# Who turns q and k, how fast the weights are rounded, and the order of the last outputs: seven edits to an attention and Fourier-mixing kernel

## The chip, the cores and the metric

The kernel runs on one core of one Trainium2 chip. The metric is the device time of one execution in microseconds (us). A core has five engines that run side by side [...]: TensorE (PE in the profile) multiplies matrices, VectorE (DVE), ScalarE (ACT) and GpSimd (POOL) do elementwise work, and SyncE (SP) issues the DMA transfers. Each engine takes its instructions in program order, so one that waits holds up everything queued behind it on the same engine.

## The reference, cut to what matters

Two stages follow each other. The first is block-sparse attention over 4 batches of 8 heads, 768 positions and 64 features per head; the mask lets a query block of 32 positions see its neighbours, the first and last block, and three random blocks.

```python
scores = scale * np.matmul(q, k.transpose(0, 1, 3, 2))
scores = np.where(mask, scores, -1000000000.0)
attn = np.exp(scores - np.max(scores, axis=-1, keepdims=True))
attn = attn / (np.sum(attn, axis=-1, keepdims=True) + 1e-09)
attn_out = np.matmul(attn, v)
x = attn_out.transpose(0, 2, 1, 3).reshape(B, S, H * D)      # 4 x 768 x 512
u = x + np.real(np.fft.fft(np.fft.fft(x, axis=1), axis=2))
un = (u - mean(u)) / np.sqrt(var(u) + 1e-06)                 # over the 512 columns
out = u + np.maximum(un @ w_ch1, 0.0) @ w_ch2                # 512 -> 2048 -> 512
```

The two weight matrices arrive as 64-bit floats.

## The kernel before, in words

**Attention.** The heads are taken two at a time: `pairs` is 4 batches of 4 pairs, 16 in all. A pair has 12 units (two halves of the queries, six chunks of 128 keys). `slot(sl)` is the loop body and takes two units, so a pair takes six slots, a batch (a *phase*) 24, and the attention 96. In a slot, `scores` makes S = K Q^T for its two units on TensorE (line 570), `weigh` makes the exponentials on ScalarE (line 590), and `values` multiplies the exponentials of the slot before with v (line 633). Exponentials live in four buffers (`ep`), so one must be used up before the exponential four units later can be written.

**The mask** comes in two ways. Early units are in `by_pe`: two more small bf16 products per unit, of `factors["at"]`, add a large negative number to the scores (line 580). Later units multiply the exponentials by a stored mask on VectorE (line 595). The switch is made by `go()` in `begin`, when the Fourier mixing of batch 0 is under way.

**The sums of the softmax** are made by TensorE in phase 0 (`add_up`, line 701). From phase 1 on `gather` adds up exponentials, either in one VectorE instruction (line 614) or in two GpSimd instructions (line 619). The two buffers it adds into are the ones that hold the two factors of the mask in phase 0; that is why `keep_factors`, in slot 19 (`sl == SB - 5`), first copies the factors into another buffer, room 2 of six (`room(i, ...)`). Before, two DMA transfers do this (line 479). Every later use of the factors reads the copy.

**Turning q and k.** The scores need q and k with the features on the partitions. Pairs up to number 4 are turned on TensorE (`turn`, line 503) and copied out of PSUM by ScalarE (lines 506, 512). Pairs from `BY_VECTOR` on (5 before) are loaded in blocks of 32 (`load_blocks`), turned by VectorE in one instruction each (`flip_blocks`, line 537) and, for q, put into order by six ScalarE copies (`in_order`, line 545). These steps stand at the end of the slot's work.

**The weights** come in 32 chunks of 128 x 512 64-bit words. A chunk is loaded into one of the six rooms (`w_load`, line 441) and rounded by two ScalarE instructions (lines 450, 453) and five VectorE instructions (lines 454, 456, 459, 461, 462). `w_steps` rounds chunks until `W_PACE * sl` are done, 1.42 a slot before, so that the last is done in slot 23; rooms 0 and 1 are wanted for the mixing afterwards.

**Mixing and channels.** `mixer` and `fourier` make the second stage of a batch while the next batch's attention runs. The steps stand in a queue, `apart`, and the large products in another, `late`. A small model of the engines' clocks (`when`, `busy`) decides at every `gap` how many of these steps are put between the attention's instructions. In `apart` are the division by the sums (line 743), the folding of x (lines 766 to 794, on VectorE), the products with the cosine and sine tables (lines 814 to 871), and the transposes back (`un_flip`, line 958). A step names the PSUM banks that it needs: `m` has two, `t` one; a capital `M` means both of `m`. The last batch makes its outputs in `outputs` (seven products a tile, line 1152) and stores them with `store` (line 1100).

The lines that carry the prediction:

```python
    BY_VECTOR = NP + 1                       # NP = 4
    W_PACE = 1.42
    ROOMS = 6
    def w_load(i):
        t = room(i % ROOMS, [P, 3 * WN], "wraw", U32)
    def w_steps(sl):
        while state["w"] < min(len(wchunks), W_PACE * sl):
            w_round(state["w"])
```

Of the kernel before, what the change touches and what calls it, by code (L numbers as in the profile page):

```python
# [102 lines left out]
def kernel(  # L103
# [14 lines left out]
    nc = tc.nc  # L118
# [91 lines left out]

    BY_VECTOR = NP + 1

    def load_blocks(n, a, tile):

# [219 lines left out]
    def room(i, shape, name, dtype=FP32):  # L436
        return big.tile(shape, dtype, tag=f"big{i}", name=name)

    def w_load(i):
        t = room(i % ROOMS, [P, 3 * WN], "wraw", U32)  # L440
        nc.sync.dma_start(out=t[:, 0:2 * WN].bitcast(I32), in_=wchunks[i][0])
        wraw[i] = t

# [25 lines left out]

    by_pe = set()
    factors = {"at": (of_k, off_q)}

    def keep_factors():

        kept = room(2, [P, 2, S], "factors", BF16)
        for a, t in enumerate(factors["at"]):
            nc.sync.dma_start(out=kept[:, a, :], in_=t)
# [104 lines left out]
    def weigh(u, s):  # L584
        n, w = divmod(u, UP)
        half, c = divmod(w, C)
        e = ep.tile([P, 2, HS], FP32, tag="e", name="e")
        e_of[u] = e
        if u in by_pe:
            nc.scalar.activation(out=e, in_=s[:, :, 0:HS], func=ACT.Exp, scale=scale)  # L590
            e_at[u] = busy("ACT", 0.8, max(s_at[u], e_free.pop(u - 2 * SLOT, 0.0))) + HOP
        else:
            nc.scalar.activation(out=s[:, :, 0:HS], in_=s[:, :, 0:HS], func=ACT.Exp, scale=scale)  # L593
            m = mask[:, c, half * HS:(half + 1) * HS].rearrange("p (o s) -> p o s", o=1)
            nc.vector.tensor_tensor(out=e, in0=s[:, :, 0:HS], in1=m.broadcast_to([P, 2, HS]),  # L595
                                    op=ALU.mult)
            e_at[u] = busy("DVE", 0.97, busy("ACT", 0.8, s_at[u]) + HOP) + HOP
            if n >= NP:
                gather(u)

    def gather(u):

# [20 lines left out]
    def values(u):  # L623
        n, w = divmod(u, UP)
        half, c = divmod(w, C)
        e = e_of[u]
        busy("PE", 0.75, e_at[u])
        vt = v_of[n]
        if c == 0:
            o_of[n, half] = ps_o.tile([P, HS], FP32, tag="o", name="o")  # L630
        o = o_of[n, half]
        for i in range(2):
            nc.tensor.matmul(o[D * i:D * i + D, :], vt[:, i, c, :], e[:, i, :],  # L633
                             start=(c == 0), stop=(c == C - 1))
        if u in by_pe and n >= NP:
            gather(u)
        if c == C - 1:
            if half == 1:
                v_of.pop(n)
            oT = sum_p.tile([P, HS], FP32, tag="oT", name="oT")  # L640
            if in_blocks(n):
                nc.vector.transpose(out=oT, in_=o_of.pop((n, half)))
                oT_at[n, half] = busy("DVE", 0.5, when["PE"] + HOP) + HOP
            else:
                nc.scalar.copy(out=oT, in_=o_of.pop((n, half)))
                oT_at[n, half] = busy("ACT", 0.5, when["PE"] + HOP) + HOP
            o_of[n, half] = oT
# [107 lines left out]
    def fourier(b, xA, xB, uns):  # L755
# [45 lines left out]
        def along(g):  # L801

            sa, sd, e1 = st["f"]
            if g == 0:
                st["zc"] = zc_p.tile([P, 2, KS], FP32, tag="zc", name="zc")
            ps = ps_m.tile([P, 512], FP32, tag="m", name="zp")
            odd = S // 4

            def cosine(ps, rows, cols):
                mm = nc.tensor.matmul
                for t in (0, 2):
                    mm(ps[rows, 0:KS], sa[:, t, cols], cs_sb[:, t, :], start=(t == 0), stop=False)  # L814
                mm(ps[rows, 0:odd], e1[:, cols], cs_sb[:, 1, 0:odd], start=False, stop=False)
                mm(ps[rows, odd:KS], sa[:, 1, cols], cs_sb[:, 1, odd:KS], start=False, stop=True)

            def keep_cosine(dst, ps):
                nc.scalar.copy(out=dst, in_=ps[:, 0:KS])

                nc.scalar.copy(out=_grid(dst, P + 1, 2, 63, 63, 1),
                               in_=_grid(ps, P, 2, 65, 63, 1))
                nc.scalar.copy(out=_run(dst, P, 2, P - 1), in_=_run(ps, P + 64, 2, -1))

            if g < 2:
                cosine(ps, slice(0, P), parts[g])
# [94 lines left out]
        def d(us, fn, *args):  # L921
# [7 lines left out]
        first += [("M" if g == 2 else "m", lambda g=g: along(g), 2.1, (1.0 if g < 2 else 0.5), 0.0)  # L929
                  for g in range(4)]  # L930
        pq = [("m", lambda m=m: across(m), 2.6 if m == 1 else 1.6, 0.7, 0.95) for m in range(T)]
        ar = [[d(1.4 if m == 1 and half == 1 else 1.0, arrive, half, m) for m in range(T)]
# [11 lines left out]
    def mixer(b, xA, xB):  # L944
# [6 lines left out]
        def un_flip(half, m):  # L951
            if half not in unT:
                unT[half] = tr_p.tile([P, ND, T * P], FP32, tag="tr", name="unT")
            un = uns.pop((half, m))
            tag, pool = (("t", ps_t), ("m", ps_m))[half]
            tp = pool.tile([P, ND, P], FP32, tag=tag, name="utp")
            for d in range(ND):
                nc.tensor.transpose(tp[:, d, :], un[:, d * P:(d + 1) * P], ident)  # L958
# [135 lines left out]
            if r == NF // 4 - 1:  # L1094
                store(half, m)

        def store(half, m):
            x = (xA, xB)[half]
            for p0, cnt, rows in _rows(out[b], T * half + m):
                nc.sync.dma_start(out=rows, in_=x[p0:p0 + cnt, m, :])  # L1100
            if m == T - 1:
                finished.add((b, half))

# [34 lines left out]
        def outputs(r, m, after):  # L1138
# [55 lines left out]
            ahead(4)  # L1194

        fl = [[("tm"[h], lambda h=h, m=m: un_flip(h, m), 0.6, 0.55, 0.0) for m in range(T)]
              for h in range(2)]

        before = first + [pq[0], ar[0][0], ar[1][0], sp[0][0],
# [44 lines left out]
    def do_apart():  # L1244
# [5 lines left out]
            return  # L1250
        done = state["ready"]
        if kind != "-":
            at = bank(kind.lower())
            done = busy("PE", pe, done) + HOP
        fn()
        if act:
# [7 lines left out]
    def gap(rest=0.0, ahead=None, kinds="tm"):  # L1264
# [4 lines left out]
        while apart:  # L1269
# [7 lines left out]
                if max(when["DVE"], state["ready"]) + dve > when["PE"] + rest + ahead:  # L1277
                    break
            elif kind != "-":
                bank_at = (max if kind == "M" else min)(free[kind.lower()])  # L1280
                if kind.lower() in used or max(state["ready"], bank_at) > when["PE"] + 0.1:
                    break
                used += kind.lower()
            do_apart()
        for item in list(short):
            kind, ready, fn = item
# [36 lines left out]
        return True  # L1323

    def w_loads():
        while state["got"] < min(len(wchunks), state["w"] + ROOMS):
            w_load(state["got"])
            state["got"] += 1

# [5 lines left out]
    def slot(sl):  # L1335
# [101 lines left out]
        while short and (not more or soon) and (  # L1437
# [159 lines left out]
```

## Time and profile before

| | |
|---|---|
| time, median of 3 | 1080.54 us (1080.32 to 1081.24) |
| span of the profiled execution | 1079.5 us |
| TensorE busy | 1042.1 us, 97% |
| VectorE busy | 661.5 us, 61% |
| ScalarE busy | 376.4 us, 35% |
| GpSimd busy | 227.4 us, 21% |
| mean granted TensorE clock | 0.991 |
| DMA, mean | 44 GB/s, but 177 to 239 GB/s in the first four fortieths |

The profile's page gives busy times, a strip of 40 slices and the costliest groups. A busy TensorE is an upper bound, since matmuls overlap and their ends are modelled. A share over the whole span hides that the stages differ: VectorE is 61% busy over all, but 95% in the first 100 us, in which the weights are rounded. The page's list of waits names, for each engine, which line of which engine ended its idle time.

### The profile page before, as it was taken

To read this page: it belongs to the slowest core of one execution; us is meant where nothing else is said; L and a number is where in the kernel's file an instruction comes from. 1 tells how busy PE (TensorE), PEld (TensorE's weight loads), DVE (VectorE), ACT (ScalarE), POOL (GpSimd) and SP (SyncE) were. 2 spreads that over 40 slices of the span, in tenths; PEclk is the share of its full clock that TensorE was granted. 3 is DMA by queue.
4 is the path that set the end of the run, shared out by engine and by line. 5 is a ranking of instruction groups with operands and counts; after the bars stand their busy time and mean duration, and the time that the engine had idled before them with its cause. 6 is when DMAs were issued, how large, how long until landed. Compare 5 with 4: busy or idle time off the path is not lost.

```text
span 1079.5 us, 12378 instructions
## 1 busy us (share of the span) xinstructions
PE 1042.1 (97%) x4378; PEld 537.1 (50%) x4378; DVE 661.5 (61%) x1226; ACT 376.4 (35%) x742; POOL 227.4 (21%) x256
## 2 busy tenths in 40 slices
PE   8999789999999999999999999999999999999996
PEld 4433234444455545444444555444444555568575
DVE  5899494777763634764568446665557255675663
ACT  5998555564311202443451302343320212210210
POOL 1000062323600001265454000354630001000000
PEclk9999899999999999999999999999999999999998
DMA  7757222221000001222211000212000001000001
GB/s 224 220 177 239 69 45 44 45 45 30 15 0 1 1 0 30 59 39 42 52 29 31 1 0 18 64 29 39 14 9 7 0 1 30 29 1 1 1 19 43
DMA packets 120769, 47.04 MB, mean 44 GB/s; under 512 B 108142, under 2 KB 113532, under 8 KB 120700
## 3 DMA queue, kind: packets, MB, share of 16 engines
q1 hardware_dynamic: 118812, 45.38, 17.1%
q10 hardware_dynamic: 1856, 0.79, 0.3%
q8 instruction: 36, 0.59, 0.2%
q14 instruction: 33, 0.27, 0.1%
q0 software_dynamic: 32, 0.01, 0.0%
HBM read 37.11 MB, written 6.29 MB: 40 GB/s over the span
## 4 chain that ended last, share of the span: by engine, by line
PE 90%; DVE 6%; issue 2%; ACT 1%; DMA 0%; POOL 0%; SPq 0%; ACTq 0%; POOLq 0%; DVEq 0%
PE y L1089 23%; PE z L1033 15%; PE s L570 12%; PE o L633 11%; PE yp L1033 8%; PE yy L1152 6%; PE xp L1033 4%; PE zp L843 2%; PE sp L701 1%; PE s L580 1%; PE zp L814 1%; PE tp L503 1%; PE utp L958 1%; PE sp L715 1%; PE xt L657 1%
## 5 line engine op out<-in xcount | busy, mean ns | idle before, releaser
L619 POOL TENSOR_TENSOR acc<-acc,e 128x384 f32<-128x384 f32 x154 | 156.8, 1055 | 212.2 <-ACT e L590 137.6
L570 PE MATMUL s<-qT,kT 64*128 64x384 f32 x768 | 154.3, 517 | 7.7 <-DVE kT L537 4.5
L633 PE MATMUL o<-e,vr 128*64 128x384 f32 x768 | 142.8, 500 | 0.0
L1092 DVE TENSOR_TENSOR x<-y,x 128x512 f32<-128x512 f32 x72 | 49.7, 690 | 133.1 <-PE y L1089 133.0
L1089 PE MATMUL y<-w_sb,hA 128*128 128x512 f32 x288 | 129.3, 596 | 1.7 <-ACT zs L845 1.7
L1089 PE MATMUL y<-w_sb,hB 128*128 128x512 f32 x288 | 128.5, 596 | 1.0 <-DVE x L1092 1.0
L595 DVE TENSOR_TENSOR e<-s,mask 128x768 f32<-128x768 f32 x98 | 89.0, 950 | 54.2 <-ACT s L593 48.5
L570 PEld LDWEIGHTS s<-qT,kT 64*128 64x128 f32 x768 | 64.6, 187 | 82.8 <-issue 26.1
L593 ACT ACTIVATE s<-s 128x768 f32<-128x768 f32 x98 | 74.3, 791 | 84.2 <-PE s L570 83.9
L1033 PE MATMUL z<-unT,t 128*128 128x384 f32 x256 | 93.2, 487 | 0.3 <-DVE hA L1038 0.3
L1089 PEld LDWEIGHTS y<-w_sb,hB 128*128 128x128 f32 x288 | 53.4, 190 | 67.7 <-issue 65.3
L590 ACT ACTIVATE e<-s 128x768 f32<-128x768 f32 x94 | 71.2, 812 | 42.6 <-PE s L580 38.6
L1089 PEld LDWEIGHTS y<-w_sb,hA 128*128 128x128 f32 x288 | 53.0, 190 | 65.5 <-issue 58.8
L906 POOL TENSOR_SCALAR st<-st 128x1 f32<-128x1 f32 x24 | 8.3, 348 | 358.8 <-DVE st L905 358.8
L633 PEld LDWEIGHTS o<-e,vr 128*64 128x64 f32 x768 | 48.3, 137 | 71.0 <-issue 67.6
L1038 DVE TENSOR_TENSOR hA<-z,hA 128x384 f32<-128x384 f32 x64 | 35.7, 557 | 77.8 <-PE z L1033 77.8
L1042 ACT ACTIVATE hA<-hA 128x384 f32<-128x384 f32 x64 | 33.4, 523 | 120.4 <-DVE hA L1038 120.3
L619 POOL TENSOR_TENSOR acc<-e 128x384 f32<-128x384 f32 x40 | 42.9, 1094 | 111.9 <-PE sp L715 85.7
L1033 PEld LDWEIGHTS z<-unT,t 128*128 128x128 f32 x256 | 48.5, 190 | 34.7 <-DVE hA L1038 1.3
L1042 ACT ACTIVATE hB<-hB 128x384 f32<-128x384 f32 x64 | 33.5, 523 | 85.9 <-DVE hB L1038 85.9
L1053 ACT COPY hA<-xp 128x384 f32<-128x384 f32 x32 | 15.3, 479 | 113.0 <-PE xp L1033 113.0
L1033 PE MATMUL xp<-unT,w_sb 128*128 128x384 f32 x128 | 47.6, 494 | 2.6 <-DVE x L1092 2.6
(204 smaller groups left out, 1430.8 us busy)
## 6 DMA issues: line engine op xcount, KB each, us to landing
wraw<-in_moe_w_ch_dram SPq DMA_DIRECT2D x32, 512.0 KB
vr<-in_v_dram SPq DMA_DIRECT2D x30, 192.0 KB
qb<-in_q_dram SPq DMA_DIRECT2D x44, 96.0 KB
kb<-in_k_dram SPq DMA_DIRECT2D x44, 96.0 KB
x<-oT SPq DMA_DIRECT2D x192, 12.0 KB
out_dram<-x SPq DMA_DIRECT2D x16, 128.0 KB
out_dram<-x SPq DMA_DIRECT2D x8, 256.0 KB
qr<-in_q_dram SPq DMA_DIRECT2D x24, 64.0 KB
```

Source lines behind the costliest of these rows:

```text
L570: nc.tensor.matmul(s[:, i, 0:HS], kT[rows, c * P:(c + 1) * P], qT[rows, queries], start=True, stop=u not in by_pe)
L590: nc.scalar.activation(out=e, in_=s[:, :, 0:HS], func=ACT.Exp, scale=scale)
L593: nc.scalar.activation(out=s[:, :, 0:HS], in_=s[:, :, 0:HS], func=ACT.Exp, scale=scale)
L595: nc.vector.tensor_tensor(out=e, in0=s[:, :, 0:HS], in1=m.broadcast_to([P, 2, HS]), op=ALU.mult)
L619: nc.gpsimd.tensor_add(out=acc[:, i, :], in0=start[:, i, :], in1=e[:, i, :])
L633: nc.tensor.matmul(o[D * i:D * i + D, :], vt[:, i, c, :], e[:, i, :], start=(c == 0), stop=(c == C - 1))
L1033: nc.tensor.matmul(to, a[:, k, :], c[:, k, :], start=(k == 0), stop=(k == ND // 2 - 1))
L1038: tt(out=to, in0=ps, in1=a, op=ALU.add)
L1042: nc.scalar.activation(out=h, in_=h, func=ACT.Relu)
L1089: nc.tensor.matmul(y, hs[0, half][:, l, m * P:(m + 1) * P], w2_sb[:, 4 * r + l, :], start=(l == 0), stop=(l == 3))
L1092: nc.vector.tensor_tensor(out=x[:, m, :], in0=y, in1=x[:, m, :], op=ALU.add)
L1152: nc.tensor.matmul(ps, a[:, k, :], c[k // 2][:, k % 2, :] if isinstance(c, list) else c[:, k, :], start=(k == 0), stop=(k == 3))
```

## The change

Seven edits are made together.

1. The two factors of the mask are copied by GpSimd instead of by DMA.
2. VectorE turns q and k from pair 2 on instead of from pair 5 on.
3. The steps of such a turn are issued right after the slot's exponentials, ahead of the mixing's steps, instead of at the end of the slot.
4. The weights are rounded at 1.1 chunks a slot. The rounding then lasts beyond the slot in which rooms 0 to 2 are needed for other things, so the last six chunks use rooms 3, 4 and 5 alone.
5. Units whose mask comes from TensorE are gathered in the order of the units across the switch.
6. Two steps of the mixing take bank `t` instead of a second bank `m`: the `side` product, and the last transposes of the second half.
7. In `outputs` the product with `o_s[m, 4]` goes ahead of the one with `a22`, and the last tile's second half is stored in two pieces of columns.

```diff
-    BY_VECTOR = NP + 1
+    BY_VECTOR = 2
...
+    w_rooms = [i % ROOMS for i in range(26)] + [3, 4, 5, 3, 4, 5]
+    def w_free(i):
+        return all(w_rooms[k] != w_rooms[i] for k in range(state["w"], i))
     def w_load(i):
-        t = room(i % ROOMS, [P, 3 * WN], "wraw", U32)
+        t = room(w_rooms[i], [P, 3 * WN], "wraw", U32)
...
         for a, t in enumerate(factors["at"]):
-            nc.sync.dma_start(out=kept[:, a, :], in_=t)
+            nc.gpsimd.tensor_copy(out=kept[:, a, :], in_=t)
...
+            if n >= NP:
+                to_gather.append(u)
...
+            gather_to(u)
...
-        if u in by_pe and n >= NP:
-            gather(u)
+        gather_to(u)
...
-                side = ps_m.tile([P, 512], FP32, tag="m", name="side")
-                at = bank("m")
+                side, at = ps_t.tile([P, 512], FP32, tag="t", name="side"), bank("t")
...
-            tag, pool = (("t", ps_t), ("m", ps_m))[half]
+            tag, pool = (("t", ps_t), ("m", ps_m))[half == 1 and m != 1]
...
+            ends = r == 1 and after is None
+            if ends:
+                store(1, m, slice(DH, DM))
             ahead(2)
-            plus(b0, product(ps_s, "s", a22, rights[4]))
-            if r == 1:
-                store(1, m)
-            ahead(3)
             p3 = product(ps_m, "m", o_s[m, 4], block(r, 1, 1))
             plus(a1, p3)
             if r == 1:
                 store(0, m)
+            ahead(3)
             ahead(4)
+            plus(b0, product(ps_s, "s", a22, rights[4]))
+            if r == 1:
+                store(1, m, slice(0, DH if ends else DM))
...
-    W_PACE = 1.42
+    W_PACE = 1.1
...
         for u, ps in got:
             weigh(u, ps)
+        if BY_VECTOR <= n + 1 < len(pairs):
+            for at, fn, args in ((0, squares, (n + 1, 0)), (1, flip_blocks, (n + 1, 0)),
+                                 (2, in_order, (n + 1,)), (4, flip_blocks, (n + 1, 1)),
+                                 (5, squares, (n + 1, 1))):
+                if s == at:
+                    fn(*args)
...
-        if BY_VECTOR <= n + 1 < len(pairs):
-            for at, fn, args in ((0, squares, (n + 1, 0)), (1, flip_blocks, (n + 1, 0)),
-                                 (2, in_order, (n + 1,)), (4, flip_blocks, (n + 1, 1)),
-                                 (5, squares, (n + 1, 1))):
-                if s == at:
-                    fn(*args)
         w_loads()
         w_steps(sl)
```

More of the change, by code (lines that the diff above doesn't have):

```diff
@@ L463, in w_round @@
         busy("DVE", 3.0, busy("ACT", 1.2))
-    by_pe = set()
+    by_pe, to_gather = set(), deque()
     factors = {"at": (of_k, off_q)}
@@ L597, in weigh, with gather_to @@
             e_at[u] = busy("DVE", 0.97, busy("ACT", 0.8, s_at[u]) + HOP) + HOP
+            gather_to(u)
             if n >= NP:
                 gather(u)
+    def gather_to(u):
+        while to_gather and to_gather[0] <= u:
+            gather(to_gather.popleft())
     def gather(u):
@@ L928, in fourier @@
                  d(1.0, fold_1, 1), d(1.2, fold_2, 0), d(0.6, fold_2, 2), d(1.3, fold_2, 1)]
-        first += [("M" if g == 2 else "m", lambda g=g: along(g), 2.1, (1.0 if g < 2 else 0.5), 0.0)
+        first += [("mt" if g == 2 else "m", lambda g=g: along(g), 2.1, (1.0 if g < 2 else 0.5), 0.0)
                   for g in range(4)]
@@ L1095, in channels, with store @@
                 store(half, m)
-        def store(half, m):
+        def store(half, m, cols=slice(0, DM)):
             x = (xA, xB)[half]
-            for p0, cnt, rows in _rows(out[b], T * half + m):
-                nc.sync.dma_start(out=rows, in_=x[p0:p0 + cnt, m, :])
+            for p0, cnt, rows in _rows(out[b][:, cols], T * half + m):
+                nc.sync.dma_start(out=rows, in_=x[p0:p0 + cnt, m, cols])
             if m == T - 1:
@@ L1193, in outputs @@
                 store(0, m)
+            ahead(3)
             ahead(4)
-        fl = [[("tm"[h], lambda h=h, m=m: un_flip(h, m), 0.6, 0.55, 0.0) for m in range(T)]
+            plus(b0, product(ps_s, "s", a22, rights[4]))
+            if r == 1:
+                store(1, m, slice(0, DH if ends else DM))
+        fl = [[("tm"[h == 1 and m != 1], lambda h=h, m=m: un_flip(h, m), 0.6, 0.55, 0.0)
+               for m in range(T)]
               for h in range(2)]
@@ L1252, in do_apart @@
         if kind != "-":
-            at = bank(kind.lower())
+            at = bank(kind[0])
             done = busy("PE", pe, done) + HOP
@@ L1279, in gap @@
             elif kind != "-":
-                bank_at = (max if kind == "M" else min)(free[kind.lower()])
-                if kind.lower() in used or max(state["ready"], bank_at) > when["PE"] + 0.1:
+                bank_at = max(min(free[k]) for k in kind)
+                if (any(k in used for k in kind) or
+                        max(state["ready"], bank_at) > when["PE"] + 0.1):
                     break
-                used += kind.lower()
+                used += kind
             do_apart()
@@ L1325, in w_loads @@
     def w_loads():
-        while state["got"] < min(len(wchunks), state["w"] + ROOMS):
+        while state["got"] < len(wchunks) and w_free(state["got"]):
             w_load(state["got"])
```

## The prediction

> **What bounds the kernel now.** I read the page first: TensorE is busy 97% of the span, so time can only come from TensorE work removed or TensorE idle time removed.
>
> ```profile
> PE 1042.1 (97%) x4378; PEld 537.1 (50%) x4378; DVE 661.5 (61%) x1226; ACT 376.4 (35%) x742; POOL 227.4 (21%) x256
> PE   8999789999999999999999999999999999999996
> PEclk9999899999999999999999999999999999999998
> ```
>
> The strip shows idle time at the start (slice 1), in slices 5 and 6, and at the very end. TensorE's list of waits names the middle ones:
>
> ```profile
> PE s L580 <- DMA factors<-at_q: 9.2, 1, 9.2
> PE s L570 <- DVE kT L537: 4.5, 1, 4.5
> PE xp L1033 <- DVE x L1092: 2.6, 3, 1.8
> ```
>
> The first is the copy of the factors by DMA, the second a turned k that VectorE delivers late. After 165 us all waits together are under 9 us. The table of windows shows how the early stage is limited:
>
> ```profile
> 80.00:100.00 20.00, 19.61 (x137) 7.83 (x137) 19.02 (x48) 17.29 (x37) 0.00 (x0) 1.00 0.73 227
> 100.00:120.00 20.00, 10.84 (x63) 3.82 (x61) 10.41 (x23) 7.29 (x17) 0.00 (x0) 0.77 0.54 169
> 140.00:160.00 20.00, 17.82 (x109) 7.49 (x107) 17.66 (x26) 11.36 (x21) 15.38 (x12) 1.00 0.19 42
> ```
>
> (Columns: stretch, length, busy us of PE, PEld, DVE, ACT, POOL, then clock, DMA share, GB/s.) In phase 0 TensorE, VectorE and ScalarE are all 86 to 98% busy; at 140 us GpSimd joins and ScalarE relaxes. TensorE's timeline gives the two stalls:
>
> ```profile
> 37.10 1.56 PE L570 MATMUL s<-qT,kT 64*128 64x384 f32 x8
> ...
> 104.92 1.56 PE L570 MATMUL s<-qT,kT 64*128 64x384 f32 x8
> 115.64 0.82 PE L580 MATMUL s<-factors 64*128 64x384 bf16 x4 [9.16 <-DMA factors<-at_q]
> 116.39 2.83 PE L633 MATMUL o<-e,vr 128*64 128x384 f32 x8
> ...
> 162.35 2.93 PE L570 MATMUL s<-qT,kT 64*128 64x384 f32 x8 [4.53 <-DVE kT L537]
> ```
>
> Slots 6 to 20 start at 37.10 and 104.92: 4.84 us a slot. After each stall the matmuls run slow (line 633: 2.83 us, elsewhere 1.51). Around them the other engines:
>
> ```profile
> 110.17 0.69 DVE L462 TENSOR_TENSOR w_sb<-w_sb,wraw 128x512 f32<-128x512 f32 x1
> 111.50 0.60 SPq L479 DMA_DIRECT2D factors<-at_q  x1
> 142.49 6.24 POOL L619 TENSOR_TENSOR acc<-acc,e 128x384 f32<-128x384 f32 x6 [137.41 <-ACT e L590]
> 152.42 1.76 DVE L614 TENSOR_TENSOR acc<-acc,e 128x768 f32<-128x768 f32 x1
> 153.56 10.18 POOL L619 TENSOR_TENSOR acc<-acc,e 128x384 f32<-128x384 f32 x6 [0.20 <-ACT e L590]
> ```
>
> Room 2 is free at 110.86, when its chunk is rounded; the DMAs end only before 115.64. And six GpSimd adds take 6.24 us alone but 10.18 us beside a busy VectorE, whose own add takes 1.76 us there and 0.94 us alone.
>
> [...] the granted clock is 0.50 from 111 us on, and the work between line 580 and the next slot takes 5.56 us where 0.33 + 1.44 + 0.78 + 0.37 = 2.92 us is usual. [...] here 3.5 us pass from the end of the second issue (112.10) to the matmul.
>
> **The change part by part.**
>
> *A, phase 0.* Pairs 2 to 4 leave TensorE: 36 transposes fewer, at 0.16 us (0.48 us for three in the chain of waits), 5.8 us, all in slots 6 to 23. I summed each engine's instructions over these 18 slots from the two programs, with the mean durations of this trace. TensorE falls from 84.0 to 78.2 us (4.67 to 4.35 a slot). VectorE falls from 85.7 to 77.7: a chunk costs 0.419 + 0.692 + 0.427 + 0.692 + 0.692 = 2.92 us and there are about 0.32 fewer a slot, against two turns of about 1.0 and 1.5 us a pair. ScalarE falls by a tenth. Before, the 18 slots took 98.2 us (37.1 to 135.3), less 11.8 for the stall: 86.4, or 3% over TensorE's sum. With TensorE and VectorE equal, I expect the same 3%: 80.5, a gain of 5.8. But now ScalarE's ordering copies wait for VectorE's turn, and exponentials stand behind them; I take 1.3 off: **-4.5** (-7 to -1). DMA in blocks is more packets, but fewer weights a slot; hidden as before.
>
> *B, the factors.* Before: 9.16 idle plus 5.56 - 2.92 = 2.64 of slow clock, 11.8 us. After, GpSimd's copies still wait for VectorE to round the chunk in room 2 (chunk 20, in the same slot 19). Counting from the end of slot 19's scores: ScalarE and VectorE finish chunk 19 at 2.1, then 0.6 of table copies and 1.0 of turning q, then 2.92 for chunk 20: 6.6. TensorE gets there at 0.48 + 1.44 + 0.78 + 1.49 = 4.2. No row shows the copy. [...] I take 1.0 each: ready at 8.6, a stall of 4.4 to 4.7, and 1.7 of slow clock as after the 4.53 us stall. Together 6.4: **-5.4** (-8 to -3). Queued behind the waiting line 580 are all of the slot's scores, so exponentials and everything else wait too.
>
> *C, slots 24 to 36.* Seven chunks (20.4 us of VectorE, 9.7 of ScalarE) now fall where GpSimd gathers. Before, these 12 slots took 60.2 us (135.3 to 195.5) for 53.5 us of TensorE work: 6.7 idle, of which 4.53 + 1.65 (slow clock) are the late k. After, the mixing starts about five slots later and TensorE's work is 43.6 us. Ahead of the turn of k that slot 30 needs, VectorE has five chunks 14.6, sums and reciprocals 1.65, one q 1.0, the turn 1.5, and about 2.9 left over from slots 21 to 23: 21.6 us alone. In 147 to 164 us VectorE did 9.4 us of work in 14.5 us beside GpSimd, so 18 us of GpSimd add some 6: slot 30 starts 27.5 us after slot 24, against 22.3 of TensorE work (and 27.0 before). From there to the next k another 19.3 us of VectorE, with 21 us of GpSimd beside it: 26.5, against 21.3. GpSimd has 16 gathers of two adds at 1.05 to 1.7 us, 34 to 54 us, which points the same way. So 54 us for 43.6: 10.4 idle, **+3.7** (-6 to +12). Issuing the turn ahead of the folds (edit 3) is why it isn't more.
>
> *D.* The switch to the stored mask comes ten units later: 20 small products more at 0.082 us, **+1.65**, on TensorE's path; ten VectorE multiplies of 0.95 fewer, beside other work.
>
> *E, banks, order of gathering, turns in later phases.* The waits they touch are under 5 us in all (2.6 for xp, 1.7 for y behind zs); the rest of the instructions is the same. **-0.5** (-3 to +3).
>
> *F, the end.* VectorE ends at 1070.49 and the span at 1079.5: 9 us behind the last store. Before, the last tile stores 256 KB at 1068.8 and 256 KB at 1070.5 in two DMAs; after, only one of 128 KB comes last. Most of the 9 us is latency: **-1** (-2.5 to 0).
>
> Sum: -4.5 - 5.4 + 3.7 + 1.65 - 0.5 - 1 = -6.05, so 1080.5 - 6 = **1074.5 us**.
>
> **The rivals.** *R1: [...] slower.* Rounding weights beside GpSimd costs 12 us or more instead of 3.7, the last six chunks in three rooms also keep ScalarE waiting for DMA, and A gives 3: -3 - 5.4 + 14 + 1.65 - 1 = about +6, 1086. For it: the 1.76 against 0.94 us. Against it: TensorE needs only two turns of k from VectorE there. *R2: the overhang is hidden.* The turns come in time and GpSimd keeps pace, idle time in slots 24 to 36 falls to 1 us, C is -5.7: 1065. For it: edit 3 puts turns first. Against it: the seven chunks are ahead of them all the same. *R3: no change.* The copies are no faster than the DMA because room 2 is late, and C takes back A: 1080.
>
> **How the numbers follow.** The case worked out (1070 to 1078): 0.48. R2: 0.27. R3: 0.11. R1: 0.14. That makes faster 0.75, within 0.2% 0.11, slower 0.14. The range 1063 to 1083 takes in most of R2 and R3 and leaves out R1's and R2's far ends, about 2 in 10.
>
> **What would show each step.** A: slots 6 to 20 at about 4.5 us. B: a wait of line 587 for GpSimd of 4 to 5 us. C: waits of scores for a turned k or of exponentials for GpSimd's adds between 120 and 190 us, about 10 us in all, and rounding instructions of over 1 us there. D: 128 small products instead of 108. F: the span ends 8 us after the last VectorE instruction. The forecast is wrong if slots 24 to 36 show little idle time, or more than 15 us of it.

## The result and the profile after

| | before | after |
|---|---|---|
| time, median | 1080.43 us (1079.89 to 1081.24) | 1084.23 us (1083.53 to 1084.84) |
| ratio | | 1.0034, interval 1.0017 to 1.0052 |
| span of the profiled execution | 1079.5 us | 1081.4 us |
| mean granted TensorE clock | 0.991 | 0.984 |

The change makes the kernel slower by 0.34%, where 6 us of gain were forecast. The page of the kernel after (busy us, share, instructions; then slices of 27 us):

```profile
PE 1041.4 (96%) x4362; PEld 536.6 (50%) x4362; DVE 667.2 (62%) x1220; ACT 374.5 (35%) x727; POOL 237.0 (22%) x262
PE   8998978998999999999999999999999999999996
PEclk9998979999999999999999999999999999999998
```

TensorE's busy time hardly fell (1042.1 before) although it has 16 instructions fewer, because more of them ran at a slow clock (0.984 on average instead of 0.991). Where slices 5 and 6 were the low ones before (7 and 8 tenths), slices 4, 6, 7 and 10 are now (8, 7, 8 and 8), and the clock is low in slices 4 and 6. TensorE's list of waits after (total, times, longest):

```profile
PE s L587 <- POOL factors L486: 4.8, 1, 4.8
PE s L577 <- DVE e L604: 4.2, 2, 3.3
PE s L577 <- DVE kT L544: 4.1, 1, 4.1
PE s L577 <- ACT e L597: 4.0, 3, 3.5
PE st L741 <- DVE r L749: 3.9, 1, 3.9
```

The wait of 9.2 us for the factors became one of 4.8, the one for the turned k stayed (4.5 before), and three more of 3.3 to 3.9 us came, two of them for VectorE. Matmuls behind such waits ran slow: in the timeline below eight score products took 2.93 us behind the wait of 4.1, and 1.56 in slots 6 and 20. The table of windows after (stretch, length, busy PE, PEld, DVE, ACT, POOL, clock, DMA share, GB/s):

```profile
80.00:100.00 20.00, 19.02 (x131) 7.53 (x127) 19.06 (x45) 15.53 (x28) 0.00 (x0) 1.00 0.80 203
100.00:120.00 20.00, 16.18 (x99) 5.95 (x99) 12.52 (x27) 12.52 (x24) 1.59 (x2) 0.83 0.45 123
120.00:140.00 20.00, 15.54 (x95) 6.89 (x93) 19.38 (x29) 13.82 (x27) 12.02 (x10) 0.89 0.37 92
140.00:160.00 20.00, 15.92 (x79) 6.36 (x75) 19.35 (x28) 11.74 (x19) 9.83 (x8) 0.77 0.44 93
```

From 120 to 160 us VectorE is busy for 38.7 of 40 us, in only 57 instructions, while GpSimd is busy for half of it; the clock is 0.89 and 0.77, where the kernel before had 1.00 from 140 to 160 us. TensorE's timeline after shows where the slots stand and what the stalls are:

```profile
35.88 1.56 PE L577 MATMUL s<-qT,kT 64*128 64x384 f32 x8
...
97.46 1.56 PE L577 MATMUL s<-qT,kT 64*128 64x384 f32 x8
103.82 0.82 PE L587 MATMUL s<-factors 64*128 64x384 bf16 x4 [4.80 <-POOL factors L486]
...
137.35 0.87 PE L741 MATMUL st<-ident,sums 128*128 128x128 f32 x3 [3.94 <-DVE r L749]
...
154.62 2.93 PE L577 MATMUL s<-qT,kT 64*128 64x384 f32 x8 [4.08 <-DVE kT L544]
...
267.09 1.78 PE L577 MATMUL s<-qT,kT 64*128 64x384 f32 x8 [3.33 <-DVE e L604]
```

Slots 6 and 20 start at 35.88 and 97.46: 4.40 us a slot. Slot 30 starts at 154.62, after the stall for the turned k. With the starts of all the slots read in this way from both timelines, the 1.9 us between the two profiled spans split as follows:

| stretch | before, us | after, us | difference |
|---|---|---|---|
| start to slot 0 | 9.3 | 8.1 | -1.2 |
| slots 0 to 6 | 27.8 | 27.8 | 0 |
| slots 6 to 20 | 67.8 | 61.6 | -6.2 |
| slot 20 to 21 (the stall for the factors) | 16.3 | 11.1 | -5.2 |
| slots 21 to 24 | 14.1 | 12.7 | -1.4 |
| slots 24 to 54 | 295.4 | 313.7 | +18.3 |
| slot 54 to the end | 648.8 | 646.4 | -2.4 |

Up to slot 24 the change gains 14.0 us. The 1.2 us of the first row are not its doing: in the twelve profiles of this document slot 0 starts anywhere from 8.0 to 9.4 us. Then 18.3 are lost. The stretch from 24 to 54 holds the same work in both kernels, apart from the seven chunks of rounding, 20 small products more and ten multiplications by the stored mask fewer; otherwise only the place of the mixing between these slots differs. Slots 24 to 36 alone take 63.3 us instead of 60.3, but with less of the mixing in them, so their loss is larger than these 3 us; the part on the prediction works it out.

### The profile page after: what moved, and what is told of

The parts are those of the page before. It is cut to its first block, busy times and chain, and to the rows that moved or that the text cites. A ratio compares the mean times of both kernels' runs of the same rounds, so it can differ in the third digit from the quotient of the medians.

```text
span 1081.4 us, 12324 instructions
## 1 busy us (share of the span) xinstructions
PE 1041.4 (96%) x4362; PEld 536.6 (50%) x4362; DVE 667.2 (62%) x1220; ACT 374.5 (35%) x727; POOL 237.0 (22%) x262
## 4 chain that ended last, share of the span: by engine, by line
PE 89%; DVE 6%; issue 2%; ACT 1%; POOL 1%; DVEq 0%; POOLq 0%; ACTq 0%
PE y L1101 23%; PE z L1045 15%; PE s L577 12%; PE o L647 11%; PE yp L1045 7%; PE yy L1164 7%; PE xp L1045 4%; PE zp L855 2%; PE sp L714 1%; PE s L587 1%; DVE t L1007 1%; PE zp L827 1%; DVE w_sb L463 1%; PE utp L970 1%; DVE wraw L468 1%
## 5 line engine op out<-in xcount | busy, mean ns | idle before, releaser
L633 POOL TENSOR_TENSOR acc<-acc,e 128x384 f32<-128x384 f32 x154 | 159.1, 1067 | 88.4 <-DVE e L604 69.7
L604 DVE TENSOR_TENSOR e<-s,mask 128x768 f32<-128x768 f32 x88 | 80.0, 949 | 50.2 <-ACT s L602 40.4
L602 ACT ACTIVATE s<-s 128x768 f32<-128x768 f32 x88 | 66.7, 792 | 90.0 <-PE s L577 89.8
L597 ACT ACTIVATE e<-s 128x768 f32<-128x768 f32 x104 | 78.8, 808 | 54.6 <-PE s L587 42.3
L1101 PEld LDWEIGHTS y<-w_sb,hB 128*128 128x128 f32 x288 | 53.3, 190 | 67.8 <-issue 65.2
L633 POOL TENSOR_TENSOR acc<-e 128x384 f32<-128x384 f32 x44 | 47.9, 1109 | 129.2 <-PE sp L728 92.7
```

The source lines that it names most:

```text
L633: nc.gpsimd.tensor_add(out=acc[:, i, :], in0=start[:, i, :], in1=e[:, i, :])
L1101: nc.tensor.matmul(y, hs[0, half][:, l, m * P:(m + 1) * P], w2_sb[:, 4 * r + l, :], start=(l == 0), stop=(l == 3))
```

## Experiments

T1 is the theory that the loss is the rounding that hangs over into slots 24 to 36 (edit 4). T1a is its form in which the harm comes of GpSimd's adds, which then run beside the rounding and make its instructions longer. The rivals are that the chunks are simply too much work ahead of k, whatever GpSimd does, and that the loss comes of something else: the later switch of the mask, the turns on VectorE, the place of the turns. All runs in one table (the kernel before took 1080.9 us beside runs 1 to 4, 1080.8 beside 5 to 8 and 1081.0 beside 9 and 10; the last three columns are read from TensorE's timeline of each profiled execution):

| run | time, us | ratio to before, interval | slot 24 at | slots 24 to 54 | 54 to end |
|---|---|---|---|---|---|
| before | 1080.43 | | 135.3 | 295.4 | 648.8 |
| after | 1084.23 | 1.0034 (1.0017 to 1.0052) | 121.3 | 313.7 | 646.4 |
| 1: before, GpSimd copy | 1077.47 | 0.9970 (0.9958 to 0.9981) | 131.3 | 296.8 | 648.3 |
| 2: after, six chunks not rounded | 1072.31 | 0.9924 (0.9908 to 0.9941) | 121.9 | 301.7 | 646.4 |
| 3: after, 14 GpSimd adds left out | 1075.50 | 0.9950 (0.9933 to 0.9967) | 122.5 | 304.7 | 647.9 |
| 4: after, copy in slot 22 | 1079.44 | 0.9986 (0.9977 to 0.9995) | 116.6 | 313.9 | 646.5 |
| 5: after, pace 1.42 | 1078.66 | 0.9982 (0.9975 to 0.9988) | 133.3 | 296.6 | 647.7 |
| 6: after, turns from pair 5 on | 1087.97 | 1.0066 (1.0049 to 1.0083) | 129.2 | 310.8 | 647.0 |
| 7: after, turns at the slot's end | 1091.17 | 1.0097 (1.0080 to 1.0114) | 124.1 | 310.4 | 655.4 |
| 8: pace 1.42, pair 5, slot 22 | 1068.74 | 0.9891 (0.9875 to 0.9908) | 123.2 | 297.0 | 646.3 |
| 9: pace 1.42, slot 22 | 1074.18 | 0.9940 (0.9926 to 0.9954) | 127.1 | 296.7 | 646.3 |
| 10: before, copy in slot 22 | 1069.99 | 0.9899 (0.9884 to 0.9914) | 122.8 | 296.6 | 648.3 |

One column says most of it: slots 24 to 54 take 295 to 297 us in all six kernels that round at 1.42 chunks a slot, and 310 to 314 in the four that round at 1.1 with nothing left out, whatever else they do.

**Run 1, the GpSimd copy alone.** In the kernel before:

```diff
-            nc.sync.dma_start(out=kept[:, a, :], in_=t)
+            nc.gpsimd.tensor_copy(out=kept[:, a, :], in_=t)
```

> The kernel before with edit 1 alone: GpSimd copies the factors. Theory (edit 1 pays by itself what step B of the prediction said): the 9.2 us wait falls to about 5 to 6 us (room 2 is free 4.4 us after TensorE gets there, plus two copies of 0.8 us), the slow clock after it shrinks by about 1 us, and the time falls by 4 to 5 us, to about 1075.5 us, with slots 24 to 36 as before. Rival (the time won by the stall is lost again at the switch to phase 1, whatever the other edits): the wait falls but the time stays within 2 us of 1080.4.

The gain is 3.4 us. The wait for the factors falls from 9.2 to 6.1 us and slot 20 to 21 from 16.3 to 12.8. The copy is faster than the DMA, but it leaves more of a stall than the 4.8 us of the kernel after.

**Run 2, the overhanging chunks not rounded.** In the kernel after, for chunks 26 to 31 the five VectorE instructions are left out, and one ScalarE copy of the chunk's upper words stands for them; the two ScalarE instructions of the rounding and the rest of the work are kept, so these weights are not the right ones.

```diff
+        if i >= 26:
+            nc.scalar.copy(out=dst, in_=hi.bitcast(FP32))
+            busy("DVE", 3.0, busy("ACT", 1.2))
+            return
         nc.vector.tensor_scalar(out=a, in0=a, scalar1=3, scalar2=0x7FFFFFFF,
```

> The changed kernel with the last six weight chunks not rounded (left out: the seven rounding instructions of chunks 26 to 31, one ScalarE copy stands in, so the output of the channels is not the reference's). Theory T1 (rounding that falls beside GpSimd's adds is what slots 24 to 36 pay for): these 12 slots fall from 63.3 us to about 50, the waits for a turned k and for the reciprocals' st (4.1 and 3.9 us) go away, and the time is about 1072 us. Rival T2 (the turns by VectorE and the gathers on GpSimd alone are too much there): the slots stay at 60 us or more and the time at 1081 or more.

11.9 us less than the kernel after, and slots 24 to 54 are shorter by 12.0. Its list of waits of TensorE:

```profile
PE s L581 <- ACT e L601: 5.1, 5, 3.5
PE s L591 <- POOL factors L490: 4.8, 1, 4.8
PE s L581 <- DVE e L608: 4.2, 2, 3.3
```

(Four lines are added above, so L587 is L591 here.) The waits for the turned k and for the reciprocals are gone. The one for the factors stays, and so does the 3.3 us at the switch of the mask: T1 holds for 12 of the 18 us.

**Run 3, GpSimd's adds left out.** Of the 18 adds that the kernel after makes for pair 4 between slots 24 and 30, 14 are left out, so the sums of this pair are incomplete; all chunks are rounded.

```diff
-            for i in range(2):
+            for i in range(2 if n != NP or c == 1 else 0):
                 nc.gpsimd.tensor_add(out=acc[:, i, :], in0=start[:, i, :], in1=e[:, i, :])
```

> The changed kernel with GpSimd's adds of pair 4 left out but for the first of each half (slots 24 to 29; the sums of that pair are wrong, and so its part of the output); VectorE's instructions and all orders are kept. Theory T1a [...]: with GpSimd silent the rounding instructions of slots 25 to 30 take 0.42 and 0.69 us again instead of 1.11 and 1.37, slot 30 starts about 25 us after slot 24 instead of 33, and the time falls by 6 to 9 us to about 1077. Rival T1b (VectorE has too many instructions there even at full speed): their durations do not change, slot 30 still starts 31 us or more after slot 24, and the time falls by less than 3 us.

8.7 us less, with every chunk still ahead of the turn of k; slot 30 starts 25.3 us after slot 24 instead of 33.3, and in run 2 it is 23.5. So most of what the overhang costs is not VectorE's work alone but the meeting of this work with GpSimd's adds. The exponentials that wait for an add to give back their buffer are no rival for this gain: in the kernel after, both such waits (3.6 and 3.7 us) come behind slot 30, and they stay in run 3. The trace shows how the adds do it. First VectorE in the kernel after, under a run of eight adds (start, duration, instruction):

```profile
129.13 9.61 POOL L633 TENSOR_TENSOR acc<-acc,e 128x384 f32<-128x384 f32 x8 [1.94 <-ACT e L597]
129.31 1.11 DVE L461 TENSOR_SCALAR wraw<-wraw 128x512 uint32<-128x512 uint32 x1
...
130.46 1.37 DVE L463 SCALAR_TENSOR_TENSOR w_sb<-wraw 128x512 uint32<-128x512 uint32 x1
131.86 1.11 DVE L466 TENSOR_SCALAR wraw<-w_sb 128x512 uint32<-128x512 uint32 x1
...
133.01 1.37 DVE L468 TENSOR_TENSOR wraw<-wraw 128x512 f32<-128x512 f32 x1
134.41 1.36 DVE L469 TENSOR_TENSOR w_sb<-w_sb,wraw 128x512 f32<-128x512 f32 x1
135.70 0.96 DVE L544 STREAM_TRANSPOSE qb<-qb 128x768 f32<-128x768 f32 x1
```

One chunk takes 1.11 + 1.37 + 1.11 + 1.37 + 1.36 = 6.32 us where it takes 2.92 alone. The transpose behind it takes its usual 0.96. The reciprocals for which TensorE waited until 137.35 stand behind it. The same lines in run 3, where two adds are left at this place:

```profile
125.66 0.41 DVE L461 TENSOR_SCALAR wraw<-wraw 128x512 uint32<-128x512 uint32 x1
125.96 2.41 POOL L633 TENSOR_TENSOR acc<-e 128x384 f32<-128x384 f32 x2 [21.40 <-ACT e L597]
126.11 1.41 DVE L463 SCALAR_TENSOR_TENSOR w_sb<-wraw 128x512 uint32<-128x512 uint32 x1
127.55 1.11 DVE L466 TENSOR_SCALAR wraw<-w_sb 128x512 uint32<-128x512 uint32 x1
128.69 0.69 DVE L468 TENSOR_TENSOR wraw<-wraw 128x512 f32<-128x512 f32 x1
129.42 0.69 DVE L469 TENSOR_TENSOR w_sb<-w_sb,wraw 128x512 f32<-128x512 f32 x1
```

Two adds slow exactly two instructions, each by about the same 0.7 us whatever its own length (0.69 to 1.41, 0.43 to 1.11), and the next ones run as usual. At 139 us in the same trace two more adds do the same (0.69 to 1.37, 0.43 to 1.11). So the price did not grow with the instruction's own length: 0.72 and 0.68 us on 0.69 us of work, 0.68 on 0.43. Nor did it go by the number of inputs: alone, L461 with one input takes 0.42 us where L463 with two takes 0.69 for as many elements, and in the kernel after, under the eight adds, both took 0.7 us more (1.11 and 1.37). What in the chip holds such an instruction up, no run here shows.

The slowing goes both ways. Single adds of the kernel after, the second one beside the L463 of 130.46, and an add of the kernel before beside a fold of x, which takes 1.75 us alone:

```profile
130.09 1.18 POOL L633 TENSOR_TENSOR acc<-acc,e 128x384 f32<-128x384 f32 x1
131.24 1.45 POOL L633 TENSOR_TENSOR acc<-acc,e 128x384 f32<-128x384 f32 x1
154.10 2.54 DVE L766 TENSOR_TENSOR sa<-x 128x1536 f32<-128x1536 f32 x1
155.00 2.51 POOL L619 TENSOR_TENSOR acc<-acc,e 128x384 f32<-128x384 f32 x1
```

A VectorE instruction of 0.42 or 0.69 us that met an add here took some 0.7 us more, and the fold 0.79 (2.54 for 1.75), and the add lasted about as long as the VectorE instruction takes alone plus 0.75 us: 1.18 beside one of 0.42, 1.45 beside one of 0.69, 2.51 beside the fold, where it takes 1.00 by itself. (The delay of 0.7 is shorter than a whole add.) So, of the instructions measured here, the long ones met few adds in a given time, and the short ones many.

**Run 4, the copy of the factors three slots later.**

```diff
-        if sl == SB - 5:
+        if sl == SB - 2:
             keep_factors()
```

> The changed kernel with the factors copied in slot 22 instead of slot 19, when the chunk in room 2 has long been rounded. Theory (the rest of stall B is the late room, not the copy): the 4.8 us wait of the mask's products for GpSimd is gone or under 1 us, slot 20 takes 4.4 us instead of 11.1, slot 24 starts 5 to 7 us earlier; the time falls by 4 to 7 us, to about 1079, if slots 24 to 36 keep their length. Rival (VectorE sets the pace of these slots anyway): the wait moves on to a turned k at slot 24 or 30 and the time falls by less than 2 us.

The wait for the factors is gone, slot 24 starts 4.7 us earlier and the time falls by 4.8. The stretch from 24 to 54 is as long as before the edit (313.9 against 313.7), so the stall at the factors and the loss behind it are two separate things, though TensorE's longest wait for the turned k grew from 4.1 to 5.5 us.

**Run 5, the old pace.**

```diff
-    w_rooms = [i % ROOMS for i in range(26)] + [3, 4, 5, 3, 4, 5]
+    w_rooms = [i % ROOMS for i in range(32)]
...
-    W_PACE = 1.1
+    W_PACE = 1.42
```

> The changed kernel with the weights rounded at 1.42 chunks a slot again, in six rooms, so that none is left for slot 24 and later. Theory T1 (the overhang of rounding is what makes the change slow, but the slower pace also gave phase 0 its gain): slots 24 to 36 fall from 63 us by 8 or more, and phase 0 becomes bound by VectorE, which has 1.42 x 2.92 us of rounding a slot plus three pairs' turns, some 93 us in slots 6 to 24 (85.4 us in the changed kernel): slot 24 starts 8 to 12 us later, and the time ends within 4 us of 1084. Rival (VectorE has no part in the pace of phase 0, TensorE's transposes alone gave the gain): slot 24 starts within 3 us of 121 and the time is about 1075.

Undoing edit 4 alone brings 5.6 us. It loses 12.0 before slot 24, since slots 6 to 20 take 69.3 us (67.8 in the kernel before) and the wait for the factors is 8.7, and gains 17.1 behind it. The switch of the mask is back at its old place too: the small products are 108, and the longest wait at the switch is 1.0 us instead of 3.3. So edit 4 costs 17 us in all behind slot 24: 12 by the overhang (run 2) and 5 by what else the slower pace moves (301.7 in run 2 against 296.6 here). Of these 5, three parts of the later switch can be seen: 1.65 of products (an estimate from 20 at 0.082 us), 2.3 of longer wait, and the slow clock behind that wait. No run moved the switch alone.

The rooms of edit 4, which this run undoes too, are no rival: from 100 to 200 us of the kernel after no wait of ScalarE for a DMA is listed.

**Run 6, turns by VectorE from pair 5 on, as before** (edit 2 undone).

```diff
-    BY_VECTOR = 2
+    BY_VECTOR = NP + 1
```

> The changed kernel with pairs 2 to 4 turned by TensorE again (edit 2 undone). Theory (slots 6 to 20 became shorter mainly through TensorE's 36 transposes, 5.8 us, and slots 24 to 36 do not hang on it since the overhang stays): slots 6 to 20 go back by about 4 us, the factors' wait shrinks by about 1 us since VectorE has one turn less ahead of the chunk, slots 24 to 36 stay over 60 us, the time is about 1087 us. Rival (the slower pace of rounding alone gave phase 0 its gain): slots 6 to 20 stay at 62 us and the time at or under 1084.

3.7 us slower than the kernel after: slots 6 to 20 take 66.4 us instead of 61.6, against which slots 24 to 54 are 2.9 shorter. At the pace of 1.1 edit 2 does what it was meant to.

**Run 7, the turns at the slot's end, as before** (edit 3 undone).

```diff
         for u, ps in got:
             weigh(u, ps)
-        if BY_VECTOR <= n + 1 < len(pairs):
-            ...
         if not paired and not late:
...
+        if BY_VECTOR <= n + 1 < len(pairs):
+            ...
         w_loads()
```

> The changed kernel with the turns at the end of the slot again (edit 3 undone). Theory (the turns wait behind the rounding chunks in either place, since a chunk of the slot before is ahead of them; the early place saves only the folds): slots 24 to 36 change by less than 3 us, the time is 1083 to 1088. Rival (the early place does harm, by putting turns ahead of masks, gathers and reciprocals): the time falls by over 3 us.

6.9 us slower than the kernel after, more than expected, and slots 24 to 36 take 67.4 us, 4.1 more instead of under 3. There are two waits for a turned k, 6.3 us in all instead of 4.1, the wait for the factors is 6.2 instead of 4.8, and the stretch behind slot 54 is 9.0 us longer. Edit 3 helps. How the steps of the mixing moved behind slot 54 was not followed further.

**Run 8, the parts that help.** The kernel after with edits 1, 3, 5, 6 and 7, the copy in slot 22, and pace, rooms and turns as before.

```diff
-    BY_VECTOR = 2
+    BY_VECTOR = NP + 1
...
-    w_rooms = [i % ROOMS for i in range(26)] + [3, 4, 5, 3, 4, 5]
+    w_rooms = [i % ROOMS for i in range(32)]
...
-    W_PACE = 1.1
+    W_PACE = 1.42
...
-        if sl == SB - 5:
+        if sl == SB - 2:
```

> Meant as a better version: edits 1, 3, 5, 6 and 7 kept, pairs up to 4 turned by TensorE and 1.42 chunks a slot as before, and the factors copied by GpSimd in slot 22, when room 2 has long been free. Theory (GpSimd's copy is only held up by the late chunk; nothing of the rest costs time): the factors' wait goes, against 9.2 us plus 2.6 of slow clock before, VectorE's backlog gives back some of it, slots 24 to 36 take 60 us or less: about 1071 us. Rival (what the wait frees is lost at the switch to phase 1, as when the copy alone was made late in the changed kernel): over 1075.

1068.74 us, the best of all: 12 us under the kernel before and 15 under the one after. TensorE's waits between 90 and 200 us are down to these:

```profile
PE sp L728 <- DVE acc L628: 3.8, 1, 3.8
PE s L577 <- ACT e L597: 0.7, 2, 0.4
PE xt L670 <- ACT oT L658: 0.5, 1, 0.5
```

Neither the factors nor a turned k is waited for. But the 3.8 us in the first line, behind slot 30, are not among the waits of the kernel before, and slots 24 to 36 take 61.2 us instead of the 60 expected.

**Run 9, run 8 with edit 2.**

```diff
-    BY_VECTOR = NP + 1
+    BY_VECTOR = 2
```

> The best version so far (1068.7) with edit 2 put back: VectorE turns q and k from pair 2 on, pace 1.42, rooms in turn, factors copied in slot 22. Theory: without the overhang, earlier turns only load VectorE further. At the pace of 1.42 chunks a slot VectorE has 1.42 x 2.92 = 4.15 us of rounding and some 0.4 us of turns in a slot, and the other work on top, so slots 6 to 20 take 69 us as in the run at that pace (69.3) instead of 67.9, and the time is 1069 to 1073: edit 2 is worth nothing or a small loss here. Rival: TensorE's 36 fewer transposes (5.8 us) show at last and the time is 1064 or less.

5.4 us slower than run 8, a little more than expected, and the rival is out. (The executions spread from 1071.8 to 1076.0 us, and the profiled one is the shortest, so the trace shows only part of the loss.) Slots 6 to 20 take 71.0 us instead of 67.8; VectorE is busy for 66.5 of them, in run 8 for 62.1. The sign of edit 2 depends on the pace: 1.42 chunks are 4.15 us of VectorE in a slot, and little room is left for the turns beside them.

**Run 10, the kernel before with the edits of runs 1 and 4 alone.**

```diff
-            nc.sync.dma_start(out=kept[:, a, :], in_=t)
+            nc.gpsimd.tensor_copy(out=kept[:, a, :], in_=t)
...
-        if sl == SB - 5:
+        if sl == SB - 2:
```

> The kernel before with the factors copied by GpSimd and in slot 22 instead of 19 (the rest untouched). Theory: the whole of the stall before (11.8 us from slot 20 to 21 over its usual length) goes, less about 3 that VectorE's backlog takes from TensorE in the slots after, as with the copy in slot 19 alone, where 3.4 came of 4 to 5 expected: 1070 to 1074, slot 24 at 125 to 128 us, no wait of the mask products for GpSimd, the wait for the turned k still 4 to 5 us. Rival: VectorE is the limit up to slot 24 (its sum is 85.7 us over slots 6 to 24 against 84.0 of TensorE), the stall only hides its backlog, and the gain is no more than with the copy in slot 19: 1077.

1069.99 us: two copies moved to another engine and three slots on take all of the stall, and slot 24 comes at 122.8, sooner than expected. TensorE's timeline of this run:

```profile
104.30 1.56 PE L570 MATMUL s<-qT,kT 64*128 64x384 f32 x8
105.70 0.49 PE L580 MATMUL s<-at_q,at_k 64*128 64x384 bf16 x4
...
108.71 1.56 PE L570 MATMUL s<-qT,kT 64*128 64x384 f32 x8
...
118.25 1.56 PE L570 MATMUL s<-qT,kT 64*128 64x384 f32 x8
119.64 0.49 PE L580 MATMUL s<-factors 64*128 64x384 bf16 x4
```

Slot 20 starts at 104.30, about as before (104.92), and slot 21 4.4 us later instead of 16.3. Line 580 reads the originals (`at_q`, `at_k`) until the copy is long done (it ends at 111.99 us), and nobody waits for the copy. Whether the DMA copy would have done as well three slots later was not run: run 10 moves the engine and the place together. Runs 8 and 10 can't be told apart by their intervals, so edits 3, 5, 6 and 7 bring at most a little at the old pace (behind slot 54 the profile shows 646.3 against 648.3 us). The wait of 4.5 us for k is there in run 10 and gone in run 8, yet slots 24 to 54 are no shorter (297.0 against 296.6): slots 30 to 36 lose again what slots 24 to 30 gain.

## Why the prediction was wrong

The mechanism that decided it was named: a stage with seven chunks of rounding beside GpSimd's adds. Its size was wrong, and the cause that the rival R1 put first, with a chance of 0.14, is what happened: rounding beside GpSimd cost 13.0 us where R1 said 12 or more. That R1's 1086 lies so near the 1084.2 measured is partly luck: it took 3 us for part A, which gained 7.6, it had no term for the stall at the switch, some 3.7, and the waits of ScalarE for DMA that it also named did not come.

*A, phase 0:* the direction and TensorE as the limit were right, the size too small. -4.5 was forecast, and slots 6 to 20 and 21 to 24 gained 7.6, beyond the range of -7 to -1, at 4.40 us a slot where "about 4.5" was asked for. Less the stall, the 18 slots took 78.7 us, within 1% of the 78.2 summed for TensorE: neither the 3% over the sum nor the 1.3 us set aside for ordering copies that hold up exponentials was needed. Run 6 confirms that the turns are part of this gain, and run 5 that the slower pace is the other part. (VectorE was less full here than the 95% given at the top for the first 100 us of the kernel before: over these it was busy 81%, and 95% holds from 80 to 100 us.)

*B, the factors:* right, in part by luck. -5.4 forecast, -5.2 measured; the stall was 4.8 where 4.4 to 4.7 was worked out. The kernel after, from slot 19's scores to the copies:

```profile
92.94 1.56 PE L577 MATMUL s<-qT,kT 64*128 64x384 f32 x8
101.35 0.69 DVE L469 TENSOR_TENSOR w_sb<-w_sb,wraw 128x512 f32<-128x512 f32 x1
102.17 0.82 POOL L486 COPY factors<-at_k 128x768 bf16<-128x768 bf16 x1 [97.07 <-DVE w_sb L469]
102.93 0.83 POOL L486 COPY factors<-at_q 128x768 bf16<-128x768 bf16 x1
```

VectorE finished the room's chunk at 102.04, 7.5 us behind the end of slot 19's scores, not 6.6; against this the two copies took 0.82 and 0.83 us where 1.0 each was taken (the author's estimate; no trace of before has such a copy), and TensorE came to the wait 4.5 us behind those scores, not 4.2. What the step didn't ask is whether the copy has to stand in slot 19 at all. Runs 4 and 10 answer: it doesn't, and the whole 11.8 us of the kernel before were to be had.

*C, slots 24 to 36:* the step that failed. The prediction put the twelve slots at 54 us, +3.7 against before. They took 63.3 us (121.3 to 184.6) for the 43.6 us of TensorE work that it had summed: 19.7 above it instead of 10.4, and +13.0 against the 6.7 before.

The wrong term is "18 us of GpSimd add some 6". From slot 24's start to slot 30's, the rounding instructions sum to 28.6 us where the durations of phase 0 give 17.9 for the same ones: 10.7 us were added, by 18 adds. Some 0.35 us for each us of GpSimd had been read from a stretch of the kernel before in which many of VectorE's instructions were long (2.54 us for a fold), so that the adds beside them were long too (2.51 us) and few. Since each add here held up one instruction by about 0.7 us, the price went by the number of meetings, and rounding, with five short instructions a chunk, met nearly every add: 16 of the 30 rounding instructions that start there are slowed by over 0.3 us, and there are 18 adds. Counted by adds, the two stretches agree: the prediction's own 5.1 us (14.5 less 9.4) fell on 8 to 10 adds, 0.5 to 0.6 us each, and here it is 0.59. Two of the five instructions in a chunk have one input, and they were slowed like the others (0.42 to 1.11 us).

Slot 30 so came 33.3 us after slot 24 instead of 27.5. Run 2 takes 9.9 of these 33.3 us away, and run 3 takes 8.0 away with all of the rounding kept.

From slot 30 to 36 it took 30.0 us where 26.5 was forecast. Only 1.6 of that goes with the rounding (28.4 in run 2). The rest goes with exponentials that wait for GpSimd's adds, 7.3 us between 120 and 200 us, for one of which TensorE waits 3.5 us; these waits are there in runs 2 and 3 too, but no run was made on them alone, so that their share is not shown.

*D, the small products:* 128 instead of 108, as said. *E:* wrong for the switch of the mask. The timeline of VectorE in the kernel after, ahead of slot 53:

```profile
263.76 0.94 DVE L628 TENSOR_TENSOR acc<-acc,e 128x768 f32<-128x768 f32 x1
264.63 0.41 DVE L1007 TENSOR_TENSOR t<-unT 128x256 f32<-128x256 f32 x1
...
265.75 0.42 DVE L1007 TENSOR_TENSOR t<-unT,t 128x256 f32<-128x256 f32 x1
266.09 1.81 DVE L604 TENSOR_TENSOR e<-s,mask 128x768 f32<-128x768 f32 x2
```

The first products with the stored mask stand behind an add and four steps of the mixing, and the next scores wait 3.3 us for them. The granted clock is then 0.50 for 3.4 us (268.8 to 272.2), which adds to the loss: three products of xp take 2.13 us there, elsewhere four take 1.45. The switch was moved by edit 4 (from slot 47 to slot 52), not by the order of gathering: with pace 1.42 and edit 5 kept, it is in slot 47 and the wait is 1.0 (run 5). The forecast priced the later switch by its small products alone. Behind slot 54 the kernel after is 2.4 us shorter, and 2 us are there between runs 8 and 10 too; which of edits 3, 5, 6 and 7 brings them was not tried (without edit 3 the stretch is 9.0 us longer, run 7).

*F, the end:* nothing came. From VectorE's last instruction to the end of the span it is 1071.93 to 1081.4, 9.5 us, where it was 9.0 and 8 was forecast. Half the bytes in the last store did not shorten it: in the three profiles without edit 7 this end takes 8.5 to 9.0 us, in the nine with it 9.4 to 10.8.

The sum of the forecast was -6.05. C was mis-sized by 9.3 us, and the stall at the switch, some 3.7 (what is left of the 18.3 us), had no term. Against these 13 us stand 3.1 that A gained beyond its term, 1.2 of chance at the start of the execution and 0.9 behind slot 54 beyond E's and F's terms; with B's 0.2 the sum is the +1.9 between the two profiled spans. The medians differ by 3.8, as the profiled execution of the kernel after was the shortest of its four and that of the kernel before a longer one.

## What to carry to other kernels

Price VectorE beside GpSimd by counting meetings, not by multiplying busy time: here each GpSimd add cost the VectorE instruction that it met some 0.7 us, so work in many short instructions (a chunk's rounding, 2.9 us alone and 6.3 under the adds) doubled, while transposes (0.96 and 1.5 us) and multiplications with an input in PSUM (0.93 to 0.96) took no longer. Before an operation that stalls is made faster, ask how late it may stand: the faster engine alone brought 3.4 us, and with the copy three slots later it was 11. And work that is spread out to relieve one stage lands in the next: look at what runs beside it there, and judge edits that trade one engine's time together, since the sign of edit 2 changed with the pace.

## What the runs showed of the hardware

- A VectorE `tensor_scalar` with a single SBUF input (128x512, 32 bits) was slowed beside GpSimd's adds by as much in time, and by more in proportion, than an instruction with two inputs: 0.42 to 1.11 us against 0.69 to 1.37 (run 3 and the kernel after).
- The slowing was mutual: a GpSimd add of 128x384, 1.00 us alone, took 1.18 us beside a VectorE instruction of 0.42, 1.45 beside one of 0.69 and 2.51 beside one of 1.75.
- VectorE multiplications of the scores in PSUM by the mask in SBUF (128x768) took 0.93 to 0.96 us in the kernel after, all 88 of them, 57 with an add of GpSimd beside them for some of their time.
- VectorE transposes of 128x768 were not slowed under the same adds: 0.97 us for q and 1.49 to 1.56 for k in the kernel after with an add beside them (16 of 28), 0.97 to 0.98 and 1.52 to 1.57 without.
- A GpSimd copy of 128x768 bf16 took 0.82 us, less than an add of half as many f32 elements (1.00 us).
- The stall of 4.1 us for the turned k cost more than itself: behind it the scores ran 2.93 us instead of 1.56, and the granted clock was 0.50 from 152.7 to 159.5 us. In the kernel after there are five such stretches between 100 and 280 us, of 6.8 us each around the waits of 4.8, 3.9 and 4.1 us and of 3.4 us behind those of 3.5 and 3.3 us.
